# Key-value products of a two-layer attention and expert kernel: the heads of a pair alternate chunk by chunk, the 64-row tail is padded to 128 rows

## The chip, the cores and the metric

The kernel runs on one core of a Trainium2 chip. A time is the device time of one execution in microseconds (us); the kernel before was run three times. The engines are named as in the profile: PE is TensorE's matmul, PEld its loading of the stationary operand, DVE is VectorE, ACT ScalarE, POOL GpSimd, SP the queue that issues the DMAs.

## What is computed

Inputs are float32 `q`, `k`, `v` of shape (8 batches, 8 heads, 576 rows, 64) and four weight matrices. Per batch and head:

```python
kv  = np.einsum('bhsd,bhse->bhde', k, v)      # 64 x 64, a sum over 576 rows
out = np.einsum('bhsd,bhde->bhse', q, kv)
rms = np.sqrt(np.mean(out * out, axis=-1, keepdims=True) + 1e-06)
x   = out / rms * g_norm                      # then (4608, 512), heads side by side
h   = x @ w_in;  x = (h * clip(h + 3, 0, 6) / 6) @ w_out        # layer 1, 2048 wide
h   = x @ w_in2; out = (h * cos(h)) @ w_out2                    # layer 2
```

## The kernel before

The tokens are worked on in nine superblocks of 512. The weights arrive as 64-bit words and are turned into float32 by ACT and DVE (`decode`, L240, with the last step on L254), then into pairs of f16 (`split`, L262 and L264). For superblock 0 the first layer is done in float32 (`plain_1` L1016, `plain_2` L1031) while the weights come in; for the others, and for layer 2, the products are done with f16 halves in a seven-product scheme (first product L841, second product L660 in layer 1 and L713 in layer 2).

The attention runs ahead of layer 1 and beside it. Its first part is the product k^T v, made for one **pair of heads** at a time in `kv_pair` (L394): 576 rows are four chunks of 128 rows and a tail of 64, so each head takes five matmuls that add up in PSUM, k being the stationary operand (64 columns) and v the moving one (64 columns). Head 0 of the pair writes PSUM partitions 0 to 63, head 1 partitions 64 to 127; in the profile these are forms `128*64` (128 rows, 64 columns of the array) and, for the tail, `64*64`. Each float32 matmul of the program shows as two weight loads and two matmuls, so a pair shows 20 of each. Two DVE copies (L412) then put the result into `kvbd`, block-diagonal. The order within a pair is: five matmuls of head 0, then five of head 1.

There are 32 pairs (8 batches, 4 pairs each). The four of batch 0 are made in the prologue, each from a buffer of its own (`kvs`, and `kv` for the first), with all tails in one tile `tail` of 64 rows (L930). The other 28 are made beside layer 1: the generator `attention` (L981) emits one when its turn comes, and then `kv_load` (L379) issues four DMAs on SP for the next one into the one buffer of pool `kv`: k and v, each as 128 rows and a 64-row tail. SP executes in order, so a DMA that waits for the buffer holds up what stands behind it. The chunk work (`chunk`, L432) transposes q (L435), multiplies it by `kvbd` (L455), norms the rows on ACT and DVE and transposes back (L481). Chunks that hold rows of two batches do L455 in two pieces of 64 rows, which go to PSUM partitions 0 to 63 and 64 to 127 and so show as `128*64` too.

The instructions of an engine stand in the order in which a scheduler put them when the program was built, and every engine works through its own in that order. In layer 2 the same pool `kv` serves as a snapshot buffer (L727).

Of the kernel before, what the change touches and what calls it, by code (L numbers as in the profile page):

```python
# [21 lines left out]

# Winograd's form of Strassen's product, C = A B in 2x2 blocks:
#   S1 = A21+A22  S2 = S1-A11  S3 = A11-A21  S4 = A12-S2
#   T1 = B12-B11  T3 = B22-B12  T2 = T3+B11  N4 = B21-T2
# products in the order issued, with the accumulator each goes to:
PRODS = (
# [28 lines left out]
def attention_moe_kernel(  # L56
# [18 lines left out]
    P = 128  # L75
# [14 lines left out]
    xt_p = ctx.enter_context(tc.tile_pool(name="xt", bufs=1))  # L90
    kv_p = ctx.enter_context(tc.tile_pool(name="kv", bufs=1))
    at_p = ctx.enter_context(tc.tile_pool(name="at", bufs=2))
# [22 lines left out]
    c3_t, gn, gs = (col() for _ in range(3))  # L115
    kvbd = const.tile([P, 2, NP, P], F32, name="kvbd")

    # ---- stages: each generator emits one stage per turn, so that consecutive
    # ---- stages, which wait on each other across engines, lie a turn apart
    active = []  # L120
# [26 lines left out]

    # ---- scales
    def pow2_scale(mx, name, squares, res, at=None):
        """[P, 1] magnitudes, or sums of squares that bound theirs -> res = (s, 1/s), s a power  # L150
        of two with s * max in [TOP, 2 TOP)."""
        pt = ps_scratch(f"pt_{name}")
        nc.tensor.transpose(out=pt[0:1, 0:P], in_=mx, identity=ident)
        m1 = col(p=1)
        nc.vector.tensor_reduce(
            out=m1, in_=pt[0:1, 0:P], axis=AX.X, op=ALU.max, apply_absolute_value=True
        )
        yield
        pb = ps_scratch(f"pb_{name}")
        nc.tensor.matmul(out=pb[:, 0:1], lhsT=ones_row, rhs=m1, start=True, stop=True)  # L160
        t = sm_p.tile([P, 1], F32, tag="sc", name=f"t_{name}")
        lo, hi = (2.0 ** -96, 2.0 ** 96) if squares else (2.0 ** -48, 2.0 ** 48)
        nc.vector.tensor_scalar(out=t, in0=pb[:, 0:1], scalar1=hi, scalar2=lo, op0=ALU.min, op1=ALU.max)
        pw = sm_p.tile([P, 1], U32, tag="pw", name=f"pw_{name}")
        if squares:
            nc.vector.tensor_scalar(
                out=pw, in0=t.bitcast(U32), scalar1=1, scalar2=0x3F800000,
                op0=ALU.logical_shift_right, op1=ALU.bitwise_and,
            )
        else:  # L170
            nc.vector.tensor_scalar(
                out=pw, in0=t.bitcast(U32), scalar1=0x7F800000, scalar2=None, op0=ALU.bitwise_and
            )
        s, inv = at or (col(), col())
        nc.vector.tensor_scalar(out=inv, in0=pw.bitcast(F32), scalar1=(2.0 ** 63 if squares else 1.0) / TOP, scalar2=None, op0=ALU.mult)
        nc.vector.reciprocal(out=s, in_=inv)
        res[name] = (s, inv)
        yield
# [19 lines left out]

    # ---- weights: float64 words -> float32 -> scaled f16 hi and lo
    def raw_load(layer, kind, i):  # L200
# [10 lines left out]
    def group_scale(layer, kind, gi):  # L211
        """The scale of the weights of pairs 2 gi and 2 gi + 1."""
        mx = col()
        nc.vector.tensor_reduce(out=mx, in_=m_w[kind, layer][:, 2 * gi:2 * gi + 2], axis=AX.X, op=ALU.max)
        yield
        s, inv = s_w[kind, layer]
        yield from pow2_scale(
            mx, f"{kind}{layer}_{gi}", True, scale, (s[:, gi:gi + 1], inv[:, gi:gi + 1])
        )
        scaled.add((kind, layer, gi))  # L220

    def group_factors(layer):
        """fac = what brings each group's products to the scale common to all."""
        ts, tt = nc.vector.tensor_scalar, nc.vector.tensor_tensor
        fs = []
        for kind in "io":
            s, inv = s_w[kind, layer]
            m, f = col(), col(NG)
            nc.vector.tensor_reduce(out=m, in_=inv, axis=AX.X, op=ALU.max)
            yield  # L230
            ts(out=f, in0=s, scalar1=m, scalar2=None, op0=ALU.mult)
            yield
            nc.vector.reciprocal(out=f, in_=f)
            least[kind, layer] = m
            fs.append(f)
        yield
        tt(out=fac[layer], in0=fs[0], in1=fs[1], op=ALU.mult)
        yield

    def decode(r, t, sq):  # L240
        """float64 words r -> float32 t; sq = the sum of their squares. The upper half of a
        float64, taken for a float32, has the upper bits of the exponent for its exponent: a
        factor brings the bias to float32's, and what lies below its range to nothing."""
        hi, lo, tu = r[:, :, 1], r[:, :, 0], t.bitcast(U32)
# [42 lines left out]
    def halves_i(layer, i):  # L287
        """The scaled f16 halves of the seven left operands of pair i."""
        key = f"i{layer}"
# [39 lines left out]
    def halves_o1(i):  # L329
        """The scaled f16 halves of the seven right operands of pair i, layer 2."""  # L330
        d = wf["o", 1, i]
# [45 lines left out]

    # ---- attention: k v of one pair of heads, then chunks of 128 tokens of all heads
    def kv_load(b, p, t=None, tail=True):  # L379
        if t is None:  # L380
            t = kv_p.tile([P, 2, 2, 5, D], F32, tag="kv", name=f"kv{b}_{p}")
        for n, src in enumerate((k, v)):
# [11 lines left out]
    def kv_pair(b, p, t, tail=None):  # L394
        ps = ps_scratch(f"kv{b}_{p}")
        for h in range(2):
            for c in range(5):
                n = P if c < 4 else 64
                if c == 4 and tail is not None:
                    kh, vh = (tail[:, m, 2 * p + h] for m in range(2))  # L400
                else:
                    kh, vh = (t[0:n, m, h, c, :] for m in range(2))
                nc.tensor.matmul(  # L403
                    out=ps[64 * h:64 * h + 64, 0:64],
                    lhsT=kh,
                    rhs=vh,
                    start=(c == 0),
                    stop=(c == 4),
                )
# [5 lines left out]
    def parts(c):  # L415
        """(batch, first row in it, first row in chunk c, rows) of the pieces of chunk c."""
        r, res = 0, []
# [74 lines left out]

    # ---- a superblock's moving operands of the first product
    xraw = {}
# [9 lines left out]
    def x_ops(layer, j):  # L504
        """Two stages per operand, in the order of the products."""
        while (layer, j) not in xraw:
# [38 lines left out]

    # ---- elementwise between the two products, on two pairs of row blocks at once
    gts = {}
    ready = []

    def relu6_part(j, gi, c, row, half):  # L550
        """c: [P, 2 pairs, 256] of row block `row` and token half `half`."""
        stt = nc.vector.scalar_tensor_tensor
# [61 lines left out]
    def cos_operands(j, gi):  # L614
        """The halves of the seven left operands of the second product."""
        busy[0] += 1
# [67 lines left out]

    # ---- second product of layer 2
    wo_s = {}
# [6 lines left out]
    def wo_load():  # L693
        """The right operand of the next product."""
        j, n = divmod(n_wo[0], 7)
# [9 lines left out]
    def prod2(j, n, mt, i, end):  # L705
# [19 lines left out]
        if n in (0, 2, 4):  # L725
            if n == 4:
                t = kv_p.tile([P, 2, 256], F32, tag="kv", name=f"sn24_{j}")  # L727
            else:
                t = kvbd[:, n // 2].rearrange("p a (b c) -> p (a b c)", c=P).rearrange("p (a c) -> p a c", a=2)
# [22 lines left out]
    def units2(j):  # L752
        """The second product's pieces of superblock j, in order."""
        res = []
# [64 lines left out]
    def group(layer, j, gi, hooks):  # L819
        """The first product for pairs 2 gi and 2 gi + 1 over superblock j."""  # L820
        nm = f"{layer}_{j}_{gi}"
# [53 lines left out]

    # -- prologue
    scratch[:] = ["t", "acc0", "acc1", "acc2", "t", "acc3", "P", "R"]
# [51 lines left out]
    q_t = {}  # L929
    tail = wi_p.tile([64, 2, H, D], F32, tag="wi", name="tail")  # L930
    kv_t[0, 0] = kv_load(0, 0, tail=False)
    for n, src in enumerate((k, v)):
        nc.sync.dma_start(out=tail[:, n], in_=src[0, :, 512:576, :].rearrange("h p d -> p h d"))
    for p in range(1, NP):
# [46 lines left out]
    def attention():  # L981
        """The rest of the attention, chunk by chunk, into the superblocks' x."""
        n_kv, n_task = NP, 0
# [25 lines left out]
    def plain_1(f):  # L1009
        """Row block f of the first product in float32."""  # L1010
        w = wf["i", 0, f // 2].rearrange("p (k f) -> p k f", k=KD)
# [124 lines left out]
```

## Time and profile before

| what | value |
|---|---|
| three runs, median (lowest to highest) | 1574.88 us (1573.76 to 1577.53) |
| the profiled execution: its span, the only time recorded of it | 1573.6 us |
| PE busy | 1546.6 us, 98% |
| DVE busy | 1227.5 us, 78% |
| ACT busy | 1052.4 us, 67% |
| DMA queue share of 16 engines | 34.6% |

The span is that of one execution on the slowest (here the only) core. PE is busy nearly throughout; how its time is made up, by kind of matmul and by stage, is what the page and the windows tell. A matmul's duration holds its passage through the array, so consecutive matmuls overlap in the records, and the distance of their starts is what each costs.

### The profile page before, as it was taken

The page shows a single profiled execution, that of the slowest core. Times are in us where ns is not written, and L with a number is a line of the kernel's source. Part 1 is how long each engine was busy: PE and PEld are TensorE (multiplying, and loading weights), DVE is VectorE, ACT ScalarE, POOL GpSimd, SP SyncE. Part 2 cuts the span into 40 slices and gives each one's busy share as a digit, 9 for nine tenths or more (in the row PEclk, how much of TensorE's full clock was granted, in tenths as well). Part 3 has the DMA queues.
Part 4 walks back from the last instruction along what each step waited for, and adds up shares of the span by engine and source line. Part 5 has one row for each costly group of instructions (what it writes and reads, how often), then busy time and mean ns, then how long its engine had stood idle before and what let it go on. Part 6 is the DMA issues. An engine that isn't in the chain of part 4 may idle for free.

```text
span 1573.6 us, 28793 instructions
## 1 busy us (share of the span) xinstructions
PE 1546.6 (98%) x11902; PEld 1179.6 (75%) x11902; DVE 1227.5 (78%) x2234; ACT 1052.4 (67%) x1714; POOL 0.7 (0%) x6
## 2 busy tenths in 40 slices
PE   7999999999999999999999999999999999999998
PEld 6444676676766766676666778888888888888887
DVE  4789876776768676967475799989898989889881
ACT  4566665665656564666355788878788888888771
POOL 0000000000000000000000000000000000000000
PEclk9999999999999999999999999999999999999999
DMA  6643422425151433312013142433334334243434
GB/s 181 220 147 109 121 94 81 135 64 171 42 167 51 129 113 100 117 34 81 21 35 114 48 154 101 141 115 128 116 127 148 127 115 155 92 151 121 143 110 157
DMA packets 112066, 180.11 MB, mean 114 GB/s; under 512 B 51008, under 2 KB 83776, under 8 KB 102720
## 3 DMA queue, kind: packets, MB, share of 16 engines
q1 hardware_dynamic: 111936, 178.28, 34.6%
q8 instruction: 93, 1.52, 0.4%
q14 instruction: 37, 0.30, 0.1%
HBM read 144.70 MB, written 33.55 MB: 113 GB/s over the span
## 4 chain that ended last, share of the span: by engine, by line
PE 55%; DVE 29%; ACT 11%; issue 2%; DMA 2%; SPq 0%; DVEq 0%
PE acc L660 20%; PE P L841 11%; DVE uA L593 5%; PE R L841 5%; DVE uA L598 5%; DVE gs_A L264 4%; PE kv L403 4%; DVE gs_S L264 4%; ACT uA L595 3%; PE h L1016 3%; PE acc L1031 3%; PE Q L841 3%; DVE c L857 2%; PE po L455 2%; ACT uA L596 2%
## 5 line engine op out<-in xcount | busy, mean ns | idle before, releaser
L841 PEld LDWEIGHTS <-wi 128*128 128x128 f16 x5712 | 557.4, 98 | 108.5 <-issue 4.9
L660 PE MATMUL acc<-g,wo 128*128 128x512 f16 x1536 | 368.6, 379 | 0.3 <-ACT g L567 0.3
L660 PEld LDWEIGHTS <-wo 128*128 128x128 f16 x1536 | 148.8, 98 | 134.7 <-issue 1.1
L841 PE MATMUL P<-xoB,wi 128*128 128x256 f16 x1536 | 190.3, 273 | 1.6 <-ACT sn L853 1.5
L841 PE MATMUL P<-xoT,wi 128*128 128x256 f16 x1536 | 189.1, 273 | 0.5 <-ACT sn L853 0.2
L713 PEld LDWEIGHTS <-gs_A 128*128 128x128 f16 x1632 | 159.7, 98 | 20.4 <-issue 1.9
L853 ACT ACTIVATE sn<-P 128x512 f32<-128x512 f32 x204 | 119.2, 584 | 70.0 <-PE P L841 69.4
L713 PEld LDWEIGHTS <-gs_S 128*128 128x128 f16 x1392 | 136.1, 98 | 22.3 <-issue 6.6
L595 ACT ACTIVATE uA<-uA,cols 128x512 f32<-128x512 f32 x144 | 103.6, 720 | 62.7 <-DVE uA L593 61.3
L554 ACT ACTIVATE u<-c,cols 128x512 f32<-128x512 f32 x96 | 77.9, 812 | 85.6 <-DVE c L857 66.2
L713 PE MATMUL P<-wo,gs_S 128*128 128x256 f16 x888 | 114.6, 273 | 5.3 <-ACT sn L732 5.3
L569 DVE TENSOR_TENSOR g<-u,g 128x512 f16<-128x512 f32 x128 | 87.6, 688 | 30.0 <-ACT g L567 29.1
L567 ACT ACTIVATE g<-u 128x512 f16<-128x512 f32 x128 | 80.1, 627 | 43.8 <-DVE u L556 43.4
L713 PE MATMUL P<-wo,gs_A 128*128 128x256 f16 x840 | 107.2, 273 | 1.6 <-ACT sn L732 1.6
L556 DVE SCALAR_TENSOR_TENSOR u<-u,cols,c 128x512 f32<-128x512 f32 x96 | 71.9, 749 | 38.1 <-ACT u L554 37.8
L262 ACT ACTIVATE gs_A<-uA,cols 128x512 f16<-128x512 f32 x125 | 88.3, 713 | 16.4 <-DVE uA L598 11.3
L264 DVE SCALAR_TENSOR_TENSOR gs_A<-uA,cols,gs_A 128x512 f16<-128x512 f32 x125 | 92.7, 747 | 7.4 <-ACT gs_A L262 5.4
L591 ACT ACTIVATE uA<-c,cols 128x512 int32<-128x512 f32 x108 | 77.2, 715 | 30.1 <-DVE c L862 21.9
L841 PE MATMUL R<-xoT,wi 128*128 128x256 f16 x768 | 94.7, 273 | 0.0
L841 PE MATMUL Q<-xoB,wi 128*128 128x256 f16 x768 | 94.6, 273 | 0.0
L841 PE MATMUL R<-xoN,wi 128*128 128x256 f16 x768 | 94.5, 273 | 0.0
L598 DVE SCALAR_TENSOR_TENSOR uA<-uA,c 128x512 f32<-128x512 f32 x108 | 74.1, 687 | 23.0 <-ACT uA L596 22.1
(203 smaller groups left out, 2298.4 us busy)
## 6 DMA issues: line engine op xcount, KB each, us to landing
wo<-wod SPq DMA_DIRECT2D x63, 1024.0 KB, 4.9
ri<-in_moe_w_in_dram SPq DMA_DIRECT2D x16, 1024.0 KB, 6.2
ro<-in_moe_w_out_dram SPq DMA_DIRECT2D x16, 1024.0 KB, 5.2
x2d<-o SPq DMA_DIRECT2D x36, 256.0 KB, 2.4
xr<-x2d SPq DMA_DIRECT2D x9, 1024.0 KB, 4.7
out_dram<-o SPq DMA_DIRECT2D x36, 256.0 KB, 3.8
q<-in_q_dram SPq DMA_DIRECT2D x30, 256.0 KB, 3.0
kv<-in_k_dram SPq DMA_DIRECT2D x29, 256.0 KB, 2.8
```

The lines of the kernel that those rows point to most:

```text
L262: nc.scalar.activation(out=hi, in_=src, func=AF.Copy, scale=s)
L264: nc.vector.scalar_tensor_tensor(out=lo, in0=src, scalar=s, in1=hi, op0=ALU.mult, op1=ALU.subtract)
L554: nc.scalar.activation(out=u, in_=c, func=AF.Relu, scale=u0[:, gi:gi + 1], bias=b0[:, gi:gi + 1])
L567: nc.scalar.activation(out=gt[:, :, 0, sl], in_=u, func=AF.Copy)
L569: nc.vector.tensor_tensor(out=gt[:, :, 1, sl], in0=u, in1=gt[:, :, 0, sl], op=ALU.subtract)
L593: stt(out=u, in0=ui, scalar=nk, in1=c, op0=ALU.mult, op1=ALU.add)
L595: nc.scalar.activation(out=u, in_=u, func=AF.Sin, scale=hf)
L598: stt(out=u, in0=u, scalar=0.5 * SIG2, in1=c, op0=ALU.subtract, op1=ALU.mult)
L660: nc.tensor.matmul(out=acc[e], lhsT=w[:, a, row, e * P:(e + 1) * P], rhs=g[:, c], start=(n == 0 and i == 0), stop=(n == NF - 1 and i == 2),)
L713: nc.tensor.matmul(out=ps[:, mt], lhsT=g[:, c, pr, mt * P:(mt + 1) * P], rhs=w[:, i, a], start=(first and k == 0), stop=(end and k == 2), ...
L841: nc.tensor.matmul(out=ps[bank][:, pr], lhsT=w[:, a, A_AT[an], kk], rhs=x[:, c, kk], start=(first and pr == 0 and i == 0 and kk == 0), sto ...
L853: nc.scalar.activation(out=sn[n], in_=ps["P"], func=AF.Copy)
```

## The change

Within `kv_pair` the loops are exchanged: chunk by chunk, head 0 then head 1. The tail is done with all 128 rows; rows 64 to 127 of the tail's place hold zeros, written once by POOL, in the tile `tail` (64 x 1024 elements) and in a buffer `kv_buf`, which takes the place of the pool `kv`: a fixed tile instead of one that is allocated anew for every pair. Comments and docstrings were blanked out as well, and line numbers move by two to six (L403 becomes L401, L455 becomes L449).

```diff
-    kv_p = ctx.enter_context(tc.tile_pool(name="kv", bufs=1))
+    kv_buf = const.tile([P, 2, 2, 5, D], F32, name="kv_buf")
...
-    def kv_load(b, p, t=None, tail=True):
-        if t is None:
-            t = kv_p.tile([P, 2, 2, 5, D], F32, tag="kv", name=f"kv{b}_{p}")
+    def kv_load(b, p, t=kv_buf, tail=True):
...
-        for h in range(2):
-            for c in range(5):
-                n = P if c < 4 else 64
+        for c in range(5):
+            for h in range(2):
                 if c == 4 and tail is not None:
                     kh, vh = (tail[:, m, 2 * p + h] for m in range(2))
                 else:
-                    kh, vh = (t[0:n, m, h, c, :] for m in range(2))
+                    kh, vh = (t[:, m, h, c, :] for m in range(2))
...
-                t = kv_p.tile([P, 2, 256], F32, tag="kv", name=f"sn24_{j}")
+                t = kv_buf[:, 0, :, 0:4, :].rearrange("p h c d -> p h (c d)")
...
-    tail = wi_p.tile([64, 2, H, D], F32, tag="wi", name="tail")
+    tail = wi_p.tile([P, 2, H, D], F32, tag="wi", name="tail")
+    nc.gpsimd.memset(tail[64:P], 0.0)
+    nc.gpsimd.memset(kv_buf[64:P, :, :, 4, :], 0.0)
...
-        nc.sync.dma_start(out=tail[:, n], in_=src[0, :, 512:576, :].rearrange("h p d -> p h d"))
+        nc.sync.dma_start(out=tail[0:64, n], in_=src[0, :, 512:576, :].rearrange("h p d -> p h d"))
```

Four places where the instructions stand otherwise follow, each before and after. A row is an instruction with its line, what it writes and reads, and how many equal ones follow each other.

PE, the first two pairs in the prologue, before (`kv_0`, `kv_1` are the PSUM results of pairs 0 and 1):

```order
L403 MATMUL kv_0_157<-kv_0_130 64x64 x4
L403 MATMUL kv_0_157<-tail 64x64
L403 MATMUL kv_0_157<-kv_0_130 64x64 x4
L403 MATMUL kv_0_157<-tail 64x64
L403 MATMUL kv_1_170<-kvs_135 64x64 x4
L403 MATMUL kv_1_170<-tail 64x64
L403 MATMUL kv_1_170<-kvs_135 64x64 x4
L403 MATMUL kv_1_170<-tail 64x64
```

and of the changed kernel, all four pairs and what follows them:

```order
L401 MATMUL kv_0_156<-kv_buf 64x64 x8
L401 MATMUL kv_0_156<-tail 64x64 x2
L401 MATMUL kv_1_169<-kvs_134 64x64 x8
L401 MATMUL kv_1_169<-tail 64x64 x2
L401 MATMUL kv_2_182<-kvs_137 64x64 x8
L401 MATMUL kv_2_182<-tail 64x64 x2
L401 MATMUL kv_3_195<-kvs_140 64x64 x8
L401 MATMUL kv_3_195<-tail 64x64 x2
L429 MATMUL pq_223<-ident,q_143 128x128 x4
```

The two tails of a pair now stand together at its end; that the eight before them alternate between the heads is seen in the loop, not in these rows.

PE, the first pair of batch 1, which is cut in two by the transposes of a chunk (`px`), before:

```order
L481 MATMUL px_341<-ident,sq_243 128x128 x4
L403 MATMUL kv_0_373<-kv_0_363 64x64 x3
L481 MATMUL px_346<-ident,sq_252 128x128 x4
L403 MATMUL kv_0_373<-kv_0_363 64x64 x7
L1016 MATMUL h_0_399<-xr_0_148,di_0_282 128x128
```

and after:

```order
L475 MATMUL px_340<-ident,sq_242 128x128 x4
L401 MATMUL kv_0_371<-kv_buf 64x64 x5
L475 MATMUL px_345<-ident,sq_251 128x128 x4
L401 MATMUL kv_0_371<-kv_buf 64x64 x5
L1012 MATMUL h_0_396<-xr_1_148,di_0_281 128x128
```

The cut moves from after the third to after the fifth matmul. Apart from this, PE's order is the same throughout, and so are DVE's and ACT's.

SP, the one place where DMAs change places (`ri`, `ro` are raw weights, of blocks 4 and 5 here; `kv_0` is the first pair of batch 2), before:

```order
L208 DMA ro_4_717<-in_moe_w_out_dram 128x2x1024
L208 DMA ri_5_763<-in_moe_w_in_dram 128x4x512
L383 DMA kv_0_664<-in_k_dram 128x2x256
L388 DMA kv_0_664<-in_k_dram 64x2x64
L383 DMA kv_0_664<-in_v_dram 128x2x256
L388 DMA kv_0_664<-in_v_dram 64x2x64
L208 DMA ro_5_790<-in_moe_w_out_dram 128x2x1024
```

and after:

```order
L208 DMA ro_4_711<-in_moe_w_out_dram 128x2x1024
L382 DMA kv_buf<-in_k_dram 128x2x256
L387 DMA kv_buf<-in_k_dram 64x2x64
L382 DMA kv_buf<-in_v_dram 128x2x256
L387 DMA kv_buf<-in_v_dram 64x2x64
L208 DMA ri_5_757<-in_moe_w_in_dram 128x4x512
L208 DMA ro_5_784<-in_moe_w_out_dram 128x2x1024
```

The load of `ri` of block 5 now stands behind the four loads of a pair, which wait for the pair before to be done.

POOL, at the start of the program, after (before, the rows without the two memsets of `tail` and `kv_buf`):

```order
masks.py:197 MEMSET ident 128x128
L925 MEMSET tail 64x1024
masks.py:199 ISA
masks.py:199 AFFINE_SELECT ident<-ident 128x128
L926 MEMSET kv_buf 64x4x64
```

The identity, which the first transposes need, is finished behind the larger of the two memsets.

## Rows read from the trace of the kernel before

**Rows 1.** Windows by stage: busy us of each engine (count), granted clock, DMA share, GB/s.

```profile
54.00:110.00 56.00, 56.00 (x202) 27.18 (x201) 49.09 (x94) 35.83 (x51) 0.00 (x0) 1.00 0.52 162
...
165.00:640.00 475.00, 473.29 (x3487) 331.29 (x3486) 348.39 (x704) 279.74 (x466) 0.00 (x0) 1.00 0.34 105
640.00:760.00 120.00, 120.00 (x836) 81.86 (x834) 92.58 (x223) 72.96 (x121) 0.00 (x0) 1.00 0.24 82
```

**Rows 2.** Timeline, PE: start, busy us; first whole pair beside layer 1, and what follows.

```profile
54.09 1.80 PE L403 MATMUL kv<-kv 128*64 128x64 f32 x20
55.82 0.70 PE L1031 MATMUL acc<-u,do 128*128 128x512 f32 x1
```

**Rows 3.** Timeline, PE: three short stretches within that pair.

```profile
54.20 0.40 PE L403 MATMUL kv<-kv 128*64 128x64 f32 x4
...
54.49 0.48 PE L403 MATMUL kv<-kv 128*64 128x64 f32 x3
...
54.70 0.32 PE L403 MATMUL kv<-kv 64*64 64x64 f32 x2
```

**Rows 4.** Line L403, all pairs beside layer 1: count, ns min/median/max, first and last start.

```profile
L403 PE MATMUL kv<-kv x560: 217/222/271, 33.4 to 636.1; 128*64 128x64 f32 x149, 64*64 64x64 f32 x38
```

**Rows 5.** Timeline, PE: L455 in pieces of 64 rows: the first 2, 4 and all 16.

```profile
99.26 0.33 PE L455 MATMUL po<-kvbd,qT 128*64 128x128 f32 x2
...
99.26 0.44 PE L455 MATMUL po<-kvbd,qT 128*64 128x128 f32 x4
...
99.26 1.09 PE L455 MATMUL po<-kvbd,qT 128*64 128x128 f32 x16
```

**Rows 6.** Timeline, PEld: the first two weight loads of the same.

```profile
99.26 0.14 PEld L455 LDWEIGHTS po<-kvbd,qT 128*64 128x64 f32 x2 [0.76 <-ACT qT L446]
```

**Rows 7.** Timeline, PE: L455 of another chunk, in one piece of 128 rows.

```profile
113.47 1.16 PE L455 MATMUL po<-kvbd,qT 128*128 128x128 f32 x8
```

**Rows 8.** Timeline, PE, prologue: start, busy us.

```profile
7.21 1.11 PE L403 MATMUL kv<-kv 128*64 128x64 f32 x8
8.25 0.47 PE L403 MATMUL kv<-tail 64*64 64x64 f32 x2
8.65 1.11 PE L403 MATMUL kv<-kvs 128*64 128x64 f32 x8
...
17.34 1.97 PE L435 MATMUL pq<-ident,q 128*128 128x128 f32 x8
```

**Rows 9.** DMAs of the prologue, issue and time to landing: last of `kvs`, then `ri`.

```profile
5.91 0.47 SPq L383 DMA_DIRECT2D kvs<-in_v_dram  x1
...
DMA to landing us min/median/max: 4.8/4.9/5.0
...
8.35 2.47 SPq L208 DMA_DIRECT2D ri<-in_moe_w_in_dram  x1
...
DMA to landing us min/median/max: 7.6/7.6/7.6
```

**Rows 10.** Timeline, ACT, prologue.

```profile
19.34 0.60 ACT L446 ACTIVATE tmp<-pq 128x512 f32<-128x512 f32 x1 [0.26 <-PE pq L435]
19.83 1.14 ACT L245 ACTIVATE di<-ri 128x1024 f32<-128x1024 f32 x1
```

**Rows 11.** The chain that ended last, by time, around 36 us.

```profile
34.50 1.39 PE kv L403 x14
...
38.27 7.56 DMA ri<-in_moe_w_in_dram
```

**Rows 12.** PE's waits from 50 to 165 us: total, times, longest.

```profile
PE h L1016 <- DVE di L254: 1.8, 1, 1.8
```

**Rows 13.** Timeline, SP and ACT: the load that changes places, and its first use.

```profile
84.76 0.37 SPq L208 DMA_DIRECT2D ri<-in_moe_w_in_dram  x1
...
98.42 1.16 ACT L245 ACTIVATE di<-ri 128x1024 f32<-128x1024 f32 x1
```

**Rows 14.** Timeline, DVE: a memset of 1024 elements in each partition.

```profile
1.18 0.91 DVE L882 MEMSET kvbd<- 128x1024 f32 x1 [0.16 <-issue]
```

More of the change, by code (lines that the diff above doesn't have):

```diff
@@ L401, in kv_pair @@
                 else:
-                    kh, vh = (t[0:n, m, h, c, :] for m in range(2))
+                    kh, vh = (t[:, m, h, c, :] for m in range(2))
                 nc.tensor.matmul(
[L404 to L408, printed above, removed]
+                    out=ps[64 * h:64 * h + 64, 0:64], lhsT=kh, rhs=vh, start=(c == 0), stop=(c == 4)
                 )
```

## The prediction

> **What bounds the kernel now.** First the windows by stage [rows 1]: from 54 to 110 us PE is busy 56.00 of 56 us, from 165 to 640 us 473.29 of 475, from 640 to 760 us 120.00 of 120, all at the full granted clock, while DVE has 12% free in the first of these stages and 27% in the second. So wherever the 28 later pairs of heads stand, matmul time is the bound, and what is taken off PE there moves all that follows, as long as no other engine becomes late. The end of that stretch runs straight into layer 2, where nothing waits for an absolute time. Second, a pair of heads on the timeline [rows 2]: it starts at 54.09 and the next work starts at 55.82, so it costs 1.73 us of PE. The line's own row [rows 4] says how many there are: 560 matmul records, 20 a pair, 28 pairs; together 48.4 us, 3% of the span. Third, what a pair is made of [rows 3]. Four matmuls of one head take 0.40 us from the first start to the last end; less the last one's own 0.22 [rows 4], that is three steps of 0.0585 us. The stretch of three that goes over into the tail takes 0.48; less 0.27 for the last (the long ones are those after a change [rows 4]) that leaves 0.21, one step of 0.0585 and one of 0.15. The two records of a tail start 0.32 - 0.22, about 0.107 us, apart. So each change of form costs 0.15 and then 0.107 where two steps would cost 0.117: 0.14 us. A pair has three inside (into the tail, into head 1, into its tail) and one at its end. Check: two runs of 0.107 + 6 x 0.0585, two tails of 0.107, four changes of 0.15 make 1.73.
>
> **Part 1, the heads alternate.** Does PE run two matmuls at once if they go to different 64 columns? This kernel already does it: L455, where a chunk spans two batches, alternates between PSUM rows 0 to 63 and 64 to 127. Its first two records end 0.33 us after the first start, the first four 0.44, all sixteen 1.09 [rows 5]. A single one of the first lasts 0.32, so the second started some 0.01 us after the first; then a step of 0.11 brings two more. Sixteen in pieces take 1.09 us where eight in one piece take 1.16 [rows 7]: the halves run side by side, and changing columns costs no drain. Their weight loads start together too: two end within 0.14 us [rows 6], hardly longer than one such load. So I take it that alternating heads run side by side, and that each head keeps its own step of 0.0585, the step of one head alone. A pair then has ten steps instead of twenty.
>
> **Part 2, the tail has 128 rows.** All matmuls of a pair have the same form, so the three changes inside go; the number of columns, and so the time of a tail, is the same. The pair costs 0.107 + 8 x 0.0585 + 0.15 at its end, 0.73 us. Saving per pair 1.73 - 0.73 = **1.00 us**; for 28 pairs 28.0. The pair that is cut in two by transposes has one entry and one exit more, before as after, and two unequal halves (six steps and four in each piece): it saves 0.9. Sum **27.9 us**. Bounds of a pair: above, that halves overlap not at all and only the changes go, 3 x 0.14 = 0.42 us, 11.9 in all; below 0.73 nothing speaks for. I take the overlap since it is seen in the same engine, form and type of data.
>
> **Part 3, the prologue.** Here four pairs stand on the path: transposes of q wait for them until 17.34, at a step of 0.107 us, half the clock (8.25 - 7.21 is 1.04 for eight, 0.40 for a tail [rows 8]). The change makes a pair 10 steps x 0.107 = 1.1 us instead of 2.9. But data sets the pace now: the last `kvs` is issued at 5.91 and lands 5.0 later, at 10.9 [rows 9]. Pair 3 then ends at 12.0 and the transposes start near 12.3, 5.1 us earlier. Next in the chain is ACT, which copies the transposes (the second at 19.34) and then decodes the first weights at 19.83 [rows 10]. The weights, `ri`, are issued at 8.35 and land 7.6 later, at 15.9 [rows 9], whatever PE does; ACT, in order, holds its squares of L455 behind that decode. So from there the shift is 19.8 - 15.9 = **3.9 us**. Bounds: 0 if a DMA not looked at is late, 5.1 if the decode didn't stand there. The shift lives on: the loads of the next weights (issued 38.27) follow on SP four loads of a pair that wait for the cut pair [rows 11], and move with it; what is late next is the same as before, PE's 1.8 us for the first decode after it [rows 12].
>
> **The small edits.** The memset of `tail` costs POOL about what DVE's of 1024 elements costs, 0.9 us [rows 14], and delays the identity, which is first used after 12 us; `kv_buf`'s has a quarter of that. Both are done before the tails land and PE needs them at 6.8; even at five times the price nothing waits. The one load of weights that goes behind four loads of a pair comes some 3 us later than at 84.76; its first use is at 98.42 [rows 13], and its landing takes some 6 to 8, so nothing waits. The fixed buffer is reused under the same wait as the pool's. Zero.
>
> **What is given back.** Between 54 and 110 us PE gains 3 us on three pairs, and DVE, 88% busy with decoding [rows 1], must follow. It has 6.9 us idle in that stretch; places where a pair gave it time to catch up (small matmuls of the weight scales wait for DVE there) may lose some. Bounds 0 and 3; I take **0.8**, since before only one wait over 0.2 us was left there. From 165 to 640 DVE has 27% free.
>
> Sum: 3.9 + 27.9 - 0.8 = 31.0 us. From the profiled span of 1573.6 that is 1542.6; the median of the runs stands 1.3 above the span, so **1543.9 us**.
>
> **A rule that speaks against it.** The rows say that PE ran sixteen half-wide matmuls from 99.26 with pairs 0.01 us apart, at a mean of 0.055 us each [rows 5]; no row shows a higher mean rate than that. The Trainium skill, "TensorE: Matmul & The Clock Gate", section "Wait — 56ns, not 53.3ns?", says that without hardware decode the sequencer spends about 62 ns on each matmul. By that page 20 matmuls would need 1.24 us and a pair would save only about 0.3 us, some 9 us in all. That is the first rival; the starts 0.01 us apart speak against a fixed interval, but they could have come from a queue that was full.
>
> **Rivals.**
> 1. *Issue is the bound.* Matmuls come no faster than the mean of the sixteen, 0.055 us [rows 5]. Then a pair costs 0.05 + 19 x 0.055 + 0.15 = 1.25 us and saves 0.5: 14 us, with the prologue (where steps are 0.107 for two, slow enough) 18 less 0.5: 1557 us. No overlap at all gives 1.31 a pair: 11.9 + 3 us, 1560. Chance 0.10.
> 2. *Others become the bound.* PE arrives 1 us early after each pair and waits for DVE, ACT or the next load, at a third of the 28 places, and loses all of the 3 us in decoding: 1544 + 9 = 1553. Against: 27% of DVE free. Chance 0.07.
> 3. *Slower: a change of columns drains the array.* Then alternating pays nine changes a pair instead of three: ten times 0.107 + 0.15 is 2.57 us, 0.84 more than now, 23.5 in all; in the prologue a group of two costs 0.40 [rows 8], 4.0 a pair instead of 2.9, 4 more: 1602 us. It decides as soon as a change of columns costs over 0.42/9 = 0.05 us without overlap. The sixteen of L455 change columns at every matmul and don't pay it [rows 5, 7]. Chance 0.04.
> 4. *Nothing to see*, losses elsewhere eat it: 0.02.
>
> **Numbers.** The forecast has 0.77; its own range is 1540 to 1549 (prologue 0 to 5, given back 0 to 3). With the first two rivals the range is 1538 to 1559, which leaves out 0.1 or a little more. About 0.3% (4.7 us) can be told from no change. Faster by more than that: forecast and rivals 1 and 2, 0.94; within it 0.02; slower 0.04.
>
> **What would show it.** On the timeline a pair beside layer 1 lasts 0.73 us to the next start instead of 1.73, records begin two by two some 0.01 us apart, and no `64*64` form is left. In the prologue the transposes of q start at 12 to 13 us, ACT's first decode at 15.9. PE's waits between 54 and 165 us stay under 3 us, and PE's busy total falls by some 30 us. Wrong it would be if the distance of starts within a pair stayed at 0.055 or more (rival 1), if the pair were short but waits of equal size followed (rival 2), or if steps of 0.15 stood between the heads (rival 3).

## The result and the profile after

| | median (lowest to highest) | runs |
|---|---|---|
| before, same chip | 1575.31 us (1573.76 to 1577.53) | 4 |
| the change | 1550.74 us (1550.16 to 1551.99) | 4 |

The ratio is 0.9845, 95% interval 0.9831 to 0.9859. The profiled execution has a span of 1549.1 us where before had 1573.6: 24.5 us less, of the 31.0 that were forecast. PE's busy time fell by 30.5 us (1546.6 to 1516.1), as forecast, and its time without work in the whole span grew by 6.0 (27.0 to 33.0).

Windows by stage of the kernel after, with the columns of [rows 1]:

```profile
54.00:110.00 56.00, 55.97 (x201) 26.64 (x201) 51.76 (x96) 36.03 (x51) 0.00 (x0) 1.00 0.56 171
165.00:640.00 475.00, 469.45 (x3624) 326.26 (x3622) 365.04 (x757) 293.84 (x488) 0.00 (x0) 1.00 0.36 112
```

Beside [rows 1], DVE went from 49.09 to 51.76 us in the first stage and kept up: PE stands still for 0.03 us there. In the second PE's time without work grew from 1.71 us to 5.55, though DVE has 23% free. This is the first sign of where the missing 6.5 us are.

A pair on the timeline of the kernel after: first the whole of it (as [rows 2]), then another pair in narrow windows that show its first 2, 4 and all 20 records:

```profile
52.29 0.80 PE L401 MATMUL kv<-kv_buf 128*64 128x64 f32 x20
53.02 0.70 PE L1027 MATMUL acc<-u,do 128*128 128x512 f32 x1
...
61.96 0.28 PE L401 MATMUL kv<-kv_buf 128*64 128x64 f32 x2
...
61.96 0.34 PE L401 MATMUL kv<-kv_buf 128*64 128x64 f32 x4
...
61.96 0.80 PE L401 MATMUL kv<-kv_buf 128*64 128x64 f32 x20
```

From 52.29 to 53.02 is 0.73 us, where [rows 2] have 1.73. Two records end 0.28 us after the first start, though one of the long ones alone lasts 0.271 (next row): the second started 0.01 us behind the first. Two more add 0.06. No row has the form `64*64` any more; the line's row, to be read beside [rows 4], says so for all 28 pairs:

```profile
L401 PE MATMUL kv<-kv_buf x560: 222/222/271, 30.3 to 611.9; 128*64 128x64 f32 x187
```

The prologue after, PE and then ACT on the timeline, beside [rows 8] and [rows 10]:

```profile
4.42 1.12 PE L401 MATMUL kv<-kv_buf 128*64 128x64 f32 x16 [4.42 <-DMA kv_buf<-in_v_dram]
...
13.15 1.97 PE L429 MATMUL pq<-ident,q 128*128 128x128 f32 x8
```

```profile
16.80 1.14 ACT L245 ACTIVATE di<-ri 128x1024 f32<-128x1024 f32 x1 [1.05 <-DMA ri<-in_moe_w_in_dram]
```

The transposes start at 13.15 instead of 17.34, ACT's first decode at 16.80 instead of 19.83, and what it waits for is the load, as forecast (for 15.9).

PE's waits from 165 to 640 us, before and after (engine, line, what it waited for: total us, times, longest):

```profile
PE P L841 <- ACT sn L853: 0.7, 1, 0.7
PE kv L403 <- DMA kv<-in_v_dram: 0.3, 2, 0.2
PE pb_x L160 <- DVE cols L155: 0.3, 1, 0.3
PE pb_o L160 <- DVE ss L466: 0.2, 1, 0.2
```

```profile
PE pb_o L160 <- DVE cols L155: 2.1, 2, 1.8
PE kv L401 <- DMA kv_buf<-in_v_dram: 0.9, 2, 0.6
PE P L835 <- ACT sn L847: 0.7, 1, 0.7
PE pb_i L160 <- DVE cols L155: 0.7, 1, 0.7
PE pt_x L153 <- DVE cols L775: 0.5, 1, 0.5
PE pb_o L160 <- DVE ss L460: 0.2, 1, 0.2
PE pb_x L160 <- DVE cols L155: 0.2, 1, 0.2
```

They sum to 1.5 us before and 5.3 after. The longest, 1.77 us at 270.34, can be followed back through three engines of the kernel after. PE, DVE, ACT and SP on the timeline, in that order:

```profile
270.34 0.38 PE L160 MATMUL pb_o<-cols,ones_row 1*128 1x1 f32 x2 [1.77 <-DVE cols L155]
```

```profile
268.82 0.69 DVE L672 TENSOR_REDUCE cols<-o 128x1 f32<-128x512 f32 x1 [1.46 <-ACT o L667]
...
270.02 0.27 DVE L155 TENSOR_REDUCE cols<-pt_o 1x1 f32<-1x128 f32 x1
```

```profile
268.10 0.69 ACT L667 ACTIVATE o<-acc,cols 128x512 f32<-128x512 f32 x1 [2.27 <-DMA x2d<-o]
```

```profile
263.81 0.34 SPq L669 DMA_DIRECT2D x2d<-o  x1
264.27 0.37 SPq L382 DMA_DIRECT2D kv_buf<-in_k_dram  x1
264.73 2.18 SPq L387 DMA_DIRECT2D kv_buf<-in_k_dram  x1
```

ACT may write an output tile `o` only when the tile's last store has landed. The store is issued at 263.81 and the loads of the next pair follow it 0.46 us later. The store took 4.2 us to land; the one at the same place before, at 274.38, had 1.56 us to the loads behind it and took 2.4:

```profile
274.38 0.34 SPq L675 DMA_DIRECT2D x2d<-o  x1
275.94 0.37 SPq L383 DMA_DIRECT2D kv<-in_k_dram  x1
```

So ACT was late, then the DVE work behind it, which is small but stands in order on DVE, then PE. ACT's waits for that store from 165 to 640 us, before and after:

```profile
ACT o L673 <- DMA x2d<-o: 0.2, 1, 0.2
```

```profile
ACT o L667 <- DMA x2d<-o: 4.0, 4, 2.3
```

A second loss stands at 47 us. After PE had been idle for 2.25 us it worked at half the granted clock. The rows are PE's timeline of the kernel after, then its windows (columns of [rows 1]):

```profile
46.88 5.37 PE L1012 MATMUL h<-xr,di 128*128 128x512 f32 x8 [2.25 <-DVE di L254]
```

```profile
44.00:47.00 3.00, 0.75 (x3) 0.15 (x2) 2.93 (x5) 1.32 (x2) 0.00 (x0) 1.00 0.37 143
47.00:50.00 3.00, 3.00 (x4) 1.16 (x5) 3.00 (x7) 2.02 (x3) 0.00 (x0) 0.54 0.27 42
```

The granted clock is 0.54 from 47 to 50 us, close to the lower of its two levels, 1.2 GHz against 2.4. Eight `h` records last 5.37 us; at the full clock they last 3.67 (shown with the last experiments). That is 1.7 us.

### The profile page after: what moved, and what is told of

Its sections match the earlier page's. It is cut to its first block, busy times and chain, and to the rows that moved or that the text cites. A ratio compares the mean times of both kernels' runs of the same rounds, so it can differ in the third digit from the quotient of the medians.

```text
span 1549.1 us, 28806 instructions
## 1 busy us (share of the span) xinstructions
PE 1516.1 (98%) x11902; PEld 1153.8 (74%) x11902; DVE 1226.3 (79%) x2234; ACT 1052.3 (68%) x1714; POOL 2.0 (0%) x8
## 3 DMA queue, kind: packets, MB, share of 16 engines
q8 instruction: 93, 1.52, 0.4%
## 4 chain that ended last, share of the span: by engine, by line
PE 51%; DVE 31%; ACT 12%; DMA 3%; issue 2%; SPq 1%; ACTq 0%
PE acc L654 18%; PE P L835 10%; DVE uA L587 5%; PE R L835 5%; DVE uA L592 4%; DVE gs_A L264 4%; DVE gs_S L264 4%; ACT uA L589 3%; PE h L1012 3%; PE Q L835 3%; PE acc L1027 3%; DVE c L851 2%; ACT uA L590 2%; PE po L449 2%; PE P L707 2%
```

## The experiments

### Which part of the change saves what

Three kernels take the change apart. Each was run beside before (1576.03 us, 7 runs).

**Alternating alone**: the heads alternate, and the tail keeps 64 rows.

```diff
-                    kh, vh = (tail[:, m, 2 * p + h] for m in range(2))
+                    kh, vh = (tail[0:64, m, 2 * p + h] for m in range(2))
...
-                    kh, vh = (t[:, m, h, c, :] for m in range(2))
+                    kh, vh = (t[0:P if c < 4 else 64, m, h, c, :] for m in range(2))
```

> The heads alternate, the tail keeps 64 rows. If halves of the array run side by side and each change of form costs 0.15 and then 0.107 us, a pair beside layer 1 has 8 records two by two, one change into the tails, and two tails side by side: 0.107 + 6 x 0.0585 / ... counted as four steps pairs of two passes: 0.46 + 0.15 + 0.107 + 0.15 = 0.87 us to the next start, against 0.73 with the padded tail; 28 x 0.13 = 3.7 us, so 1554.4 us. Rival, the tails of 64 x 64 run one after the other: 1.0 to 1.1 us a pair, 1559 to 1561 us. Rival, the padding alone brings the gain: a pair stays at 1.7 us and the time near 1575.

Measured: 1551.95 us (1551.21 to 1553.51), ratio 0.9847 [0.9832, 0.9861]. A pair takes 0.88 us from its start to the next one's. The timeline:

```profile
58.14 0.95 PE L401 MATMUL kv<-kv_buf 128*64 128x64 f32 x20
59.02 0.70 PE L1012 MATMUL h<-xr,di 128*128 128x512 f32 x1
```

The price of the pair came as expected, 0.15 us above the full change. The time is 2.4 us better than expected; the 28 pairs make 4.1 us of difference, the medians differ by 1.2. In its profile the second weight load landed in 6.1 us instead of 8.1 and the first pair beside layer 1 started at 48.33, 4.0 us earlier than in the full change; this start is taken up below.

**Padding alone**: the heads one after the other.

```diff
-        for c in range(5):
-            for h in range(2):
+        for h in range(2):
+            for c in range(5):
```

> The tail is padded, the heads one after the other. If alternation is what makes halves run side by side, a pair has 20 steps of one form: 0.107 + 18 x 0.0585 + 0.15 = 1.31 us; 28 x 0.58 = 16 us above the changed kernel, less some waits that go, 1566 us (1564 to 1568). Rival, the changes of form were all there was to gain: a pair of 0.73 us and 1551 us, as the changed kernel.

Measured: 1558.72 us (1557.26 to 1559.82), ratio 0.9887 [0.987, 0.9903]: 7 us better than expected, outside what was expected. A pair takes 1.13 us, not 1.31, which is 5 of the 7 (the other 2 were not traced):

```profile
61.18 1.20 PE L401 MATMUL kv<-kv_buf 128*64 128x64 f32 x20
62.31 0.70 PE L1012 MATMUL h<-xr,di 128*128 128x512 f32 x1
```

A stretch in the middle of the same pair, where head 0 ends and head 1 begins, has 10 records in 0.57 us:

```profile
61.41 0.57 PE L401 MATMUL kv<-kv_buf 128*64 128x64 f32 x10
```

One after the other, ten records need 9 x 0.0585 + 0.22 = 0.75 us. So three steps are missing, and 1.31 - 3 x 0.0585 is 1.13, the measured length. In the trace three times at this place two records start 4 to 6 ns apart, while the others behind the first stand a step of 0.0585 us or nearly one apart. The reading that fits is that head 1's first records started beside head 0's last; which head a record belongs to the rows don't say. What was forecast as "no overlap" has a little of it where the program changes columns within one form.

**Alternating and padded, but both heads in the same columns** (PSUM rows 0 to 63, free columns side by side), so that no two matmuls can share the array.

```diff
-                    out=ps[64 * h:64 * h + 64, 0:64], lhsT=kh, rhs=vh, start=(c == 0), stop=(c == 4)
+                    out=ps[0:64, 64 * h:64 * h + 64], lhsT=kh, rhs=vh,
+                    start=(c == 0 and h == 0), stop=(c == 4 and h == 1), skip_group_check=True,
...
-            nc.vector.tensor_copy(out=kvbd[r, b % 2, p, r], in_=ps[r, 0:64])
+            nc.vector.tensor_copy(out=kvbd[r, b % 2, p, r], in_=ps[0:64, 64 * h:64 * h + 64])
```

> Padded and alternating as in the changed kernel, but both heads go to the same 64 columns of the array (PSUM rows 0 to 63, side by side in the bank). If it takes two different halves of the columns to run side by side, a pair costs 1.31 us as without alternation, 1566 us (1564 to 1568). Rival: a matmul waits for the one before only where both add to the same accumulator, so alternation alone halves the steps: 0.73 us a pair and 1551 us.

Measured: 1564.37 us (1562.52 to 1568.17), ratio 0.9927 [0.9911, 0.9944]. A pair takes 1.31 us, as expected, so the rival (only matmuls that add to the same accumulator wait for each other) is out:

```profile
59.65 1.38 PE L401 MATMUL kv<-kv_buf 128*64 128x64 f32 x20
60.95 0.70 PE L1013 MATMUL h<-xr,di 128*128 128x512 f32 x1
```

This is the cleanest split. Same order, same forms, same number of matmuls as the change: the columns differ, and with them the PSUM rows, which go together in this program (and the start and stop flags, as the diff shows). The pair is 0.58 us longer, ten steps of 0.0585. So the overlap of two column halves is worth 0.58 us a pair and, without overlap, the three changes of form 0.42, as forecast. The two parts are not independent: alternating alone already saves 0.85 of the 1.00 (1.73 to 0.88), and the padding behind it 0.15.

### The late start beside layer 1

The profile of the change loses 1.7 us to half the clock after it waited for the second block of weights. Two kernels give that load a higher priority, so that SP issues it before the four loads that wait for the cut pair (10) or much earlier (200):

```diff
-        nc.sync.dma_start(out=dst, in_=src)
+        with tc.high_priority(10 if (layer, kind, i) == (0, "i", 1) else 0):
+            nc.sync.dma_start(out=dst, in_=src)
```

> The changed kernel, with the load of the raw weights of block 1 (and, as the scheduler then puts it, some of PE's order around 50 us) ahead of the four loads of a pair on SP. Theory: PE's half clock from 47.3 to 50.7 us follows its idle 2.25 us before the first decode of block 1, and that idle comes from the loads of a pair that stand ahead of the weights. Then the weights land 2 us earlier, the idle is under 1 us, the clock stays full, the pair after it starts at 48 to 50 instead of 52.3, and the time falls by 2 to 4 us to 1547 to 1549. Rival: the decode is late for another reason, idle and half clock stay, 1551.

> The same load moved still further ahead, before the loads of the first pair of batch 1 (16 us). Theory: the weights of block 1 lie ready before PE is done with block 0, no idle is left there, the clock stays full, and 4 us or a little more are gained: 1546 to 1547. Rival: it lengthens the prologue's loads by its own 1 MB (3 us), the chunks wait, and nothing is gained: 1550 to 1552.

Measured beside before at 1575.07 us (9 runs): 1547.33 us (1546.43 to 1549.81), ratio 0.9826 [0.9813, 0.984], and 1547.43 us (1545.7 to 1549.54), ratio 0.9825 [0.9812, 0.9838]. In the first, PE's wait ahead of the `h` matmuls is gone:

```profile
42.20 3.60 PE L1013 MATMUL h<-xr,di 128*128 128x512 f32 x8
...
45.83 0.80 PE L402 MATMUL kv<-kv_buf 128*64 128x64 f32 x20
...
47.93 1.98 PE L1028 MATMUL acc<-u,do 128*128 128x512 f32 x4
```

The pair starts at 45.83 instead of 52.29, 6.5 us earlier, and the end comes 4.4 us earlier (span 1544.7). The other 2 us were no gain: in this kernel the four `acc` records at 47.93 stand behind the pair, where the change has them ahead of it, and the next pair starts at 57.3 instead of 62.0, 4.6 us earlier. The medians are 3.4 and 3.3 us below the change's 1550.74, but the change was not run beside these two kernels; a comparison on one chip follows further down.

### A third output buffer

If the store holds up ACT, a third tile `o` must let it go (`cols` is cut from 480 to 384 columns to make room).

```diff
-    o_p = ctx.enter_context(tc.tile_pool(name="o", bufs=2))
+    o_p = ctx.enter_context(tc.tile_pool(name="o", bufs=3))
```

> The changed kernel with three buffers for evicted results instead of two (and a smaller tile of columns to make room). Theory: the later waits of PE for the weight scales (1.8, 0.7 and 0.4 us between 185 and 640 us) come from ACT, which waits for the store of the result two before, whose landing is delayed by the loads of the next pair right behind it on SP, now that the pair ends 1 us earlier; DVE's order then holds up the scale. With a third buffer ACT doesn't wait: 1 to 3 us less, 1548 to 1550. Rival: the waits come from DVE's own load, and stay: 1551.

Measured: 1548.39 us (1546.67 to 1550.29), ratio 0.983 [0.9816, 0.9843]. ACT's wait for the store falls to 0.9 us, and PE's waits from 165 to 640 us are:

```profile
PE kv L401 <- DMA kv_buf<-in_v_dram: 2.4, 2, 1.5
PE P L835 <- ACT sn L847: 0.7, 1, 0.7
PE pb_i L160 <- DVE cols L155: 0.7, 1, 0.7
PE pb_o L160 <- DVE cols L155: 0.6, 2, 0.4
PE pt_x L153 <- DVE cols L775: 0.4, 1, 0.4
PE pt_x L153 <- ACT qT L440: 0.2, 1, 0.2
```

The wait for `pb_o` fell from 2.1 to 0.6, as the chain above wants it; but the wait for a pair's loads rose from 0.9 to 2.4. The sum is 5.0 instead of 5.3. In the trace the 2.0 us by which this run ends earlier are there at the first pair already (49.90 instead of 52.29): its second weight load landed in 6.4 us. So the median within the expected range proves nothing for the buffer. Nor do the rows show that one wait turned into the other: the wait for the loads stands at 168.84 us (1.5) and 174.94 (0.9), nearly 100 us ahead of the place where `pb_o` waited. What the third buffer did change there is SP's order: a fourth store stands ahead of the pair's loads, where the change has three. On the same chip this kernel, without the early load, is 1.1 us above the one with priority 10, and their ranges overlap. Both together:

> Both: the load of block 1 far ahead, and three buffers. If both theories hold, the gains add: 1544 to 1546. If neither: 1551.

Measured: 1547.61 us (1545.65 to 1548.94), ratio 0.9825 [0.9811, 0.9838]. That is what the early load gives alone; the parts don't add, and the expected 1544 to 1546 was missed. The same once more with priority 10, run beside the change itself (before: 1575.83 us, 9 runs):

> The load of the second weights goes ahead of the four loads of a pair, and the outputs have a third buffer. In the traces the first of these starts the pairs 6 us earlier and keeps 4.4 of it; the third buffer took 1.5 us of wait for pb_o away and put 1.5 us of wait for kv_buf in its place. If that exchange is exact the median is that of the early load alone, 1547.3; if the parts add, 1545 to 1546.

Measured: 1547.62 us (1547.28 to 1548.34), ratio 0.9822 [0.9809, 0.9836]. The median is that of an exact exchange, 1547.3; the trace is not. In it `pb_o` waits 0.6 us and the pairs wait 1.3 for their loads, where the priority-10 kernel with two buffers has 2.3 and 0.4, so the kernel with the third buffer waits less there, and yet its median is no lower (the two ran on different chips). Against the change on the same chip (1550.33 us, next section) it is 2.7 us faster, and their ranges don't meet.

### Is the late start an accident?

> The changed kernel itself, once more. Theory A (the late prologue of its profile was one late DMA): in the five other runs with the same order of loads the second weight load of block `i` landed 6.1 to 6.4 us after its issue, here in 8.06; with such a landing TensorE waits 0.2 to 1.2 us for the first decode after it instead of 2.25, the granted clock stays at 1.00, and the first pair beside layer 1 starts at 48 to 51 us instead of 52.29; the span is then 1545.5 to 1547.5 and the median 1547 to 1549.5. Theory B (it belongs to the change): idle time over 2 us, half the granted clock in the matmuls that follow, the pair at 52 to 53, median 1550 to 1552.

> A third profile of the changed kernel, for the landing of the second weight load and what follows: Theory A says 6.1 to 6.5 us and a pair at 48 to 51 us, theory B 8 us and a pair at 52 to 53.

Measured: 1550.33 us (1549.53 to 1552.12), ratio 0.9842 [0.9829, 0.9856], and one time of 1549.85. Neither theory holds as it was put. (The "five other runs" of theory A are four; before, with the same order, has 7.56 us.) The load landed in 7.3 us both times; PE's rows of the two:

```profile
48.15 3.67 PE L1012 MATMUL h<-xr,di 128*128 128x512 f32 x8 [1.47 <-DVE di L254]
```

```profile
46.79 3.67 PE L1012 MATMUL h<-xr,di 128*128 128x512 f32 x8 [1.52 <-DVE di L254]
```

The clock stayed at 1.00, and the first pair came at 51.86 and 50.50. The wait is there each time (theory B) but shorter; the half clock is not. The medians, 1550.74 and 1550.33, agree with theory B.

Theory A left out two things. The landing goes with the chip: 6.1, 6.3 and 6.4 us in the three traces of one chip, 6.4 in the one of a second, 7.3, 7.3 and 7.9 in the three of a third, on which these two ran (for before, 7.56, and the change's first profile, 8.06, the chip is not known). And the load is not issued at the same time: at 34.27 us in the first profile of the change, at 36.33 and 34.92 in these two. From 19 to 25 us the granted clock is 1.00 in the first and 0.50 and 0.72 in these, and the prologue ends later in them.

To see whether idle time is what lowers the clock, two matmuls that nobody reads were put ahead of the wait:

```diff
+WARM = 2
...
+        if f == 0:
+            warm = ps_scratch("warm")
+            for n in range(WARM):
+                nc.tensor.matmul(out=warm, lhsT=w[:, 3 * P:4 * P], rhs=u, start=True, stop=True)
```

> Two matmuls of 128x512 that nobody reads (0.87 us each) ahead of the wait for the decode. If half the clock comes from the idle time, idle falls by 1.7 us, the h matmuls that follow take 3.67 us instead of 5.37, and where the load lands late 1.7 us are gained; where it lands in time (theory A), about 1 us is lost: median within 1 us of the changed kernel. If the clock falls for another reason, 5.37 us stays.

Measured: 1552.66 us (1549.69 to 1553.63), ratio 0.985 [0.9837, 0.9864]. It did not test what it was meant to. Two `acc` matmuls (four records) came to stand behind the wait in their place, the load landed in 7.9 us, and PE still stood idle for 2.05:

```profile
42.47 1.88 PE L1036 MATMUL warm<-u,do 128*128 128x512 f32 x4
...
47.26 5.37 PE L1013 MATMUL h<-xr,di 128*128 128x512 f32 x8 [2.05 <-DVE di L255]
```

The half clock is back, and the median is 2.3 us above the change's, though the ranges overlap. The cause of the lower clock is not settled by it. At this place it fell after idle stretches of 2.25 and 2.05 us and not after the stretches of 1.47 and 1.52 us here and the 1.8 of [rows 12]. Elsewhere it fell after 1.97 us at 268.05 in the alternating-alone kernel and after 2.06 at 266.47 in the one with priority 200 (0.79 from 266 to 274 us in both), and stayed at 1.00 after 1.77 at 270.34 in the change and 1.89 at 265.21 with priority 10. So the lower clock goes with the longer idle stretches in these traces; a kernel that removes the idle time at the same landing was not run.

## Why the prediction was right, and where it was off

The main forecast happened, at 1550.7 instead of 1543.9 us: inside the range of 1538 to 1559, but only because that takes in the times of the first two rivals: it is 1.7 us above the forecast's own range of 1540 to 1549 (whose bounds, prologue 0 and 3 us given back, come to 1550.0).

| term | forecast | measured in the profiled execution |
|---|---|---|
| 28 pairs | 27.9 | 27.8 (27 x 0.997, cut pair 0.9) |
| prologue, at ACT's first decode | 3.9 | 3.0 (19.83 to 16.80) |
| second weight load, landing later (8.06 us, before 7.56) | 0 | -0.5 |
| half clock after the wait | 0 | -1.7 |
| given back beside layer 1 | -0.8 | -4.5 |
| the rest | 0 | +0.4 |
| sum | 31.0 | 24.5 |

**Two matmuls at once: right, to the hundredth.** A pair is 0.73 us, as worked out from L455 and from the steps of one head. The same-column kernel shows that it is the columns (with their PSUM rows), and not the order alone, that give 0.58 of the 1.00. *Issue is the bound* (rival 1) is out: 20 records start within 0.58 us (0.80 less the last one's 0.22), 19 steps of 0.031 us in the mean, where the rival wanted 0.055. The rule of the Trainium skill, "TensorE: Matmul & The Clock Gate", section "Wait — 56ns, not 53.3ns?", is not what binds here: by its 62 ns, which it gives for the case without hardware decode, the pair would have taken 1.24 us, and the trace has 0.73. Whether hardware decode was on no run shows, so this does not contradict the page. *A change of columns drains the array* (rival 3) is out by the same rows.

**The changes of form: right.** 0.14 us each, three inside a pair: the same-column kernel is 0.42 us a pair below before. Alternating alone, which has one change more than the full change (into the tail), is 0.15 above it.

**The prologue: right in kind, 0.9 us too much.** ACT did wait for `ri`, which landed at 16.8 instead of 15.9. [Rows 9] gave 8.35 for the issue and 7.6 for the landing; both were taken as fixed "whatever PE does", and were 8.80 and 8.0.

**"What is late next is the same as before, PE's 1.8 us for the first decode after it": the step that failed.** The wait was taken as a constant. But it is the difference of a load and of the work ahead of it. Here the load landed in 8.06 us where [rows 11] have 7.56, PE waited 2.25 us, and the clock fell: 1.8 us of gain are left at the first pair (54.09 to 52.29), where 3.9 and the cut pair's 0.9 make 4.8. Of the 3.0 that are missing the prologue is 0.9 and this step the rest, 0.5 for the landing and 1.7 for the clock. In the two further profiles 2.2 and 3.6 are left.

**"What is given back", 0.8 us between 54 and 110: the term that was mis-sized, and in the wrong place.** Between 54 and 110 nothing was given back; DVE at 88% followed. From the first whole pair to the last, 580.46 us before (54.09 to 634.55) and 559.04 after (52.29 to 611.33), the gain is 21.4 us where 26 pairs at 0.997 make 25.9: 4.5 us are lost (3.6 and 5.2 in the two further profiles). PE's waits from 165 to 640 us grew by 3.8, which is most of it. "From 165 to 640 DVE has 27% free" was read as slack, but the waits there end on DMAs and on short DVE operations behind them: a pair's loads wanted 1 us earlier after each pair, and, at 268 us, a store with such loads right behind it. That these loads made the store late is argued from one place and does not hold at the next: at 358.77 a store with the loads 0.45 us behind it landed in 3.4 us, where before, at 370.90, one with 1.55 us took 4.2. *Others become the bound* (rival 2) put the loss into decoding and into 9 us; it was half that, at a handful of places and not in decoding. With a third buffer the long wait for `pb_o` was gone in each trace (0.2 us at that place), so the chain through the store is real; yet no median shows its 1.5 us, and why is open.

Open stays why the second weight load takes 6.1 to 8.1 us from one execution to the next (it goes with the chip, with one to three traces on each), and so how much of the 2.7 us between the change and the best variant is that load's place in the queue.

## What to carry to other kernels

Where a stationary operand fills only 64 columns, let consecutive matmuls write the two column halves in turn and keep them in one form: here the halves ran side by side (1.31 to 0.73 us a pair), and a tail in another form cost 0.15 us a pair more than zeros that fill it up. Price such a change by the distance of starts in a place where the kernel already does it. And when PE gets faster by a us at many places, ask of each load and store which absolute time it has, since free shares of DVE or ACT did not tell that here.

## What the runs showed of the hardware

- Two records of different column halves start 6 to 7 ns apart in the changed kernel, 20 of them within 0.58 us; in the same half they stand 0.0585 us apart.
- With the heads one after the other, a pair of one form took 1.13 us and not 1.31: three steps of 0.0585 us overlapped where the columns change. So a single change of columns helped a little, and changing at every matmul brought 0.73.
- A store of 128x512 that was followed by a pair's loads 0.46 us later landed in 4.2 us; with 1.56 us between them, in 2.4. At the next such place it was the other way round, 3.4 us and 4.2.
- The same 1 MB weight load behind the same four loads landed in 6.1 to 6.4 us in the traces of two chips, and in 7.3 to 7.9 in those of a third.
- After 2.25 and 2.05 us without work TensorE's granted clock fell to half, and eight records that take 3.67 us took 5.37; after 1.47, 1.52 and 1.8 us at the same place it stayed full.
